# Forty more matmuls on the identity in the first jobs of a fused windowed attention and soft mixture of experts

## The chip, the core and the metric

The kernel runs on one core of one Trainium2 chip. A core has TensorE (PE, matmuls, with its weight loads as PEld), VectorE (DVE), ScalarE (ACT), GpSimd (POOL) and SyncE (SP), which here issues all transfers. Each engine runs its own instructions in order; semaphores order them between engines. Matmuls write to PSUM, from which DVE and ACT copy results to SBUF; GpSimd works on SBUF alone. The metric is device time in microseconds, the median of several executions. The profile is of one execution; its span runs from the first to the last instruction.

## What is computed

Attention with a window of 128 positions and 4 sink positions, then a mixture of experts with soft slots on the attention's result, all in float32:

```python
def _attn_ref(q, k, v, n_sink, window):          # (4, 8, 768, 64) each
    scores = scale * np.matmul(q, k.transpose(0, 1, 3, 2))
    keep = is_sink | in_window
    scores = np.where(keep, scores, -1000000000.0)
    a = np.exp(scores - np.max(scores, axis=-1, keepdims=True))
    a = a / (np.sum(a, axis=-1, keepdims=True) + 1e-09)
    return np.matmul(a, v).astype(np.float32)

def _moe_ref(x, phi, w1, w2):                    # x (3072, 512), w1 (8, 512, 1024), w2 (8, 1024, 512)
    logits = x @ phi                             # 32 slots, 4 per expert
    d = softmax(logits, axis=0)
    slot_input = d.T @ x
    ...
    h = np.maximum(slot_input[e] @ w1[e], 0.0)
    slot_out[e] = h @ w2[e]
    ...
    return (softmax(logits, axis=1) @ slot_out).astype(np.float32)
```

The two softmax calls stand for the lines that are written out in the reference.

## The kernel before

**Tiling.** The attention is cut into 12 jobs: 4 batches by 3 blocks of 256 positions. A job has four score tiles (`softmax`, `tl` 0 to 3: four of the eight heads by one half of the positions in turn). For each job, `prep` transposes the block of k and of q on TensorE and has the halves copied from PSUM to `kt` and `qt` by ACT and DVE; `scores` makes a score tile in an "s" tile of PSUM; `maxima` masks it and takes the negative maxima on DVE; `exps` takes the exponentials on ACT, which gives the "s" tile back; `inverse` (DVE) and a multiplication on GpSimd normalise; `weights_transposed` transposes the weights of two tiles; ACT and DVE copy them to `xw`; `select` cuts the window's triangles out on GpSimd; `sinks_transposed`, `values` and `natural` make the block's output, and `moe.tokens` adds it to the slots' running softmax. In the first job, q and k come in quarters, and `prep` runs in two parts. `sink_values` and `batch_sinks` prepare the sinks' values (one matmul on TensorE, then work on ACT and DVE).

After the last job `moe.finish` closes the slots' softmax, and `tail` runs the experts' two layers on weights that SyncE has loaded into free buffers since the first jobs, and combines them into the output.

**Order.** The steps of `window_path` aren't issued as written. `Plan.add` records each with a key, an engine (or a choice of two), a planned time, what it reads and writes, and the PSUM tiles that it opens and closes. `Plan.order` (a list scheduler) simulates the engines with these planned times and puts each step on its engine's list: at each turn the engine that can start first takes, among the steps that could start nearly then (0.1 on TensorE), the one of the lowest key. `Plan.issue` emits the instructions in that order, and each engine keeps it.

```python
                if e == "P":
                    _, t, i = min((steps[i][0] + self.STAY * (self.modes[i] != mode), t, i)
                                  for t, i in at if t <= t0 + 0.1)
```

A step that opens PSUM tiles starts only when the banks are back. There are four "w" tiles (one bank each; transposes take two at once) and two "s" tiles. A bank comes back `LAT` = 0.25 after the planned end of the step that closes it. A change of TensorE's tile mode costs a planned `SWITCH` = 0.15.

**Fillers.** Three places issue matmuls whose results nobody reads, with counts in `WARM` (line 619). `WARM[0]` = 8 stand at the very start, before any plan (line 1155). `WARM[2]` are for the wait after the last job (lines 959 to 963). `WARM[1]` is what is changed; its steps are made at line 926, before those of the jobs, need nothing, and have key 1000, above every other key of the jobs:

```python
    def busy(e, h, n=P):
        nc.tensor.matmul(h["tile"][:, 0:n], lhsT=c.ident, rhs=c.ident[:, 0:n], start=True, stop=True)


    for _ in range(WARM[1]):
        h = plan.psum()
        add(1000.0, "P", 0.22, lambda e, h=h: busy(e, h), new=h, last=h)
```

So the planner puts one wherever TensorE has no real step within 0.1 and a "w" bank is free, from the plan's start until they are used up. A filler is a 128 by 128 by 128 product in float32: two matmul instructions and two weight loads in the trace.

Of the kernel before, what the change touches and what calls it, by code (L numbers as in the profile page):

```python
# [615 lines left out]


NSLOT = 24
WARM = 8, 10, 64
PT = 3  # L620
CFG = {'prep': [12.61, 9.18],
       'load': [-3.38, -3.85],
# [22 lines left out]
def window_path(ctx, tc, c, moe, q, k, v, phi, w1, w2, out):  # L645
# [279 lines left out]
# [5 lines that stand above are left out]
    for n, (b, j) in enumerate(jobs):  # L930
# [24 lines left out]
        if j == NJ - 1:  # L955
            if b == B - 1:
                moe.finish(plan, [t(x) for x in O["fin"]])

                for _ in range(WARM[2]):
                    h = plan.psum("s")  # L960
# [163 lines left out]
def fused(ctx, tc, q, k, v, n_sink, window, phi, w1, w2, out):  # L1124
# [28 lines left out]
    t = wps.tile([P, 512], F32, name="w")  # L1153
    for _ in range(WARM[0]):
        nc.tensor.matmul(t[:, 0:P], lhsT=c.ident, rhs=c.ident, start=True, stop=True)  # L1155
# [47 lines left out]
```

## Time and profile before

| what | us |
|---|---|
| median of 3 executions | 250.08 (249.75 to 250.85) |
| the profiled execution | 250.21 |
| its span | 248.5 |
| TensorE busy in the span | 216.5 |
| attention's jobs, about | 8 to 190 |
| last matmuls end, about | 239 |

The page gives the busy time of each engine and, in 40 slices of 6.2 us, its busy share in tenths; a row PEclk gives the TensorE clock that was granted, in tenths of the full clock. Most of the instructions carry line 127, which is the helper that keeps the program's order, so groups are told apart by the tiles that they write and read: `s<-wt,qt` are scores, `w<-ident,first` the transposes of k and q, `w<-ident` alone the fillers. Bare `wt` covers several buffers of one pool (`kt`, `xw`, weights and others).

### The profile page before, as it was taken

The page shows a single profiled execution, that of the slowest core. Times are in us where ns is not written, and L with a number is a line of the kernel's source. Part 1 is how long each engine was busy: PE and PEld are TensorE (multiplying, and loading weights), DVE is VectorE, ACT ScalarE, POOL GpSimd, SP SyncE. Part 2 cuts the span into 40 slices and gives each one's busy share as a digit, 9 for nine tenths or more (in the row PEclk, how much of TensorE's full clock was granted, in tenths as well). Part 3 has the DMA queues.
Part 4 walks back from the last instruction along what each step waited for, and adds up shares of the span by engine and source line. Part 5 has one row for each costly group of instructions (what it writes and reads, how often), then busy time and mean ns, then how long its engine had stood idle before and what let it go on. Part 6 is the DMA issues. An engine that isn't in the chain of part 4 may idle for free.

```text
span 248.5 us, 8602 instructions
## 1 busy us (share of the span) xinstructions
PE 216.5 (87%) x3356; PEld 153.7 (62%) x3356; DVE 161.5 (65%) x440; ACT 151.2 (61%) x577; POOL 142.3 (57%) x281
## 2 busy tenths in 40 slices
PE   7865899898999798999979899978999999989830
PEld 7743576675777476676747677656778434746520
DVE  3289569669899947889984888997544512215340
ACT  2167569869788886868897777988645212105230
POOL 2036687977857895976789497669984160000000
PEclk9985799999999999999999999999999999999995
DMA  5497989998799999999989997360159899996996
GB/s 123 107 203 156 173 254 285 282 277 261 224 212 280 280 254 256 266 252 191 277 177 268 282 329 165 68 214 4 44 179 370 307 384 349 348 351 222 340 331 223
DMA packets 102963, 59.44 MB, mean 239 GB/s; under 512 B 76292, under 2 KB 98820, under 8 KB 102916
## 3 DMA queue, kind: packets, MB, share of 16 engines
q1 hardware_dynamic: 102916, 58.83, 85.2%
q8 instruction: 28, 0.46, 0.8%
q14 instruction: 19, 0.16, 0.2%
HBM read 52.53 MB, written 6.29 MB: 237 GB/s over the span
## 4 chain that ended last, share of the span: by engine, by line
PE 52%; DVE 27%; ACT 13%; issue 4%; POOL 0%; ACTq 0%; DVEq 0%; POOLq 0%
PE w L127 34%; PE s L127 16%; DVE wt L127 13%; ACT wt L127 9%; DVE s L127 8%; DVE rs L127 2%; PE w L1155 2%; DVE first L127 1%; ACT wt L580 1%; ACT first L127 1%; DVE call L127 1%; DVE acc L127 1%; DVE sums L127 0%; DVE vsink L127 0%; ACT qt L127 0%
## 5 line engine op out<-in xcount | busy, mean ns | idle before, releaser
L127 ACT ACTIVATE wt<-s,wt 128x132 f32<-128x132 f32 x192 | 68.7, 377 | 10.4 <-DVE wt L127 7.2
L127 POOL TENSOR_TENSOR wt<-wt 128x528 f32<-128x528 f32 x96 | 63.9, 672 | 19.3 <-DVE wt L127 5.9
L127 POOL TENSOR_SCALAR_AFFINE_SELECT wt<-wt 128x512 f32<-128x512 f32 x88 | 54.6, 643 | 15.5 <-DVE sums L127 9.7
L127 PE MATMUL w<-wt 128*64 128x128 f32 (+3 forms) x550 | 50.6, 317 | 1.5 <-DVE wt L565 1.0
L127 PE MATMUL s<-wt,qt 64*64 64x196 f32 (+2 forms) x768 | 43.2, 332 | 9.9 <-ACT wt L127 7.0
L127 PEld LDWEIGHTS w<-wt 128*64 128x64 f32 (+2 forms) x550 | 35.9, 140 | 13.6 <-DVE wt L565 1.5
L127 ACT ACTIVATION_READ_ACCUMULATOR wt<-s,wt 128x1 f32 x192 | 40.6, 211 | 0.0
L127 PEld LDWEIGHTS s<-wt,qt 64*64 64x64 f32 x768 | 27.0, 136 | 20.0 <-ACT wt L127 10.7
L127 DVE TENSOR_REDUCE wt<-s 128x4 f32<-128x528 f32 x48 | 34.0, 707 | 1.7
L127 PE MATMUL w<-ident,wt 64*128 64x64 f32 (+1 forms) x442 | 29.3, 242 | 3.0 <-ACT wt L127 1.1
L127 ACT COPY wt<-w 128x512 f32<-128x512 f32 (+1 forms) x41 | 23.7, 581 | 11.5 <-PE w L127 8.4
L127 PEld LDWEIGHTS w<-ident,wt 64*128 64x128 f32 (+1 forms) x442 | 21.5, 144 | 12.6 <-issue 5.3
L127 DVE COPY wt<-w 128x512 f32<-128x512 f32 (+1 forms) x33 | 22.0, 667 | 10.8 <-PE w L127 10.8
L127 PEld LDWEIGHTS w<-ident,first 64*128 64x128 f32 x576 | 22.2, 143 | 10.8 <-issue 5.0
L127 PE MATMUL w<-ident,first 64*128 64x64 f32 x576 | 27.3, 234 | 1.5 <-ACT first L127 1.5
L127 ACT COPY first<-w 128x512 f32<-128x512 f32 x32 | 18.7, 593 | 15.5 <-PE w L127 15.4
L127 DVE COPY_PREDICATED s<-later,s 128x256 f32<-128x256 uint8 x48 | 20.4, 426 | 4.4 <-PE s L127 3.2
L127 DVE TENSOR_TENSOR wt<-wt 128x4 f32<-128x4 f32 x48 | 13.7, 286 | 10.2 <-ACT wt L127 9.0
L127 ACT ACTIVATE qt<-w 128x512 f32<-128x512 f32 (+1 forms) x25 | 14.4, 580 | 6.8 <-PE w L127 4.8
L127 PE MATMUL s<-wt 128*32 128x256 f32 x256 | 15.4, 381 | 1.0 <-DVE wt L565 1.0
L127 PE MATMUL w<-wt,si 128*32 128x512 f32 x112 | 13.9, 593 | 0.0
L127 POOL COPY wt<-wt 128x512 f32<-128x512 f32 (+2 forms) x13 | 5.7, 457 | 13.5 <-ACT wt L127 10.9
(115 smaller groups left out, 247.4 us busy)
## 6 DMA issues: line engine op xcount, KB each, us to landing
wt<-in_moe_w_dram SPq DMA_DIRECT2D x30, 1024.0 KB, 8.2
wt<-in_v_dram SPq DMA_DIRECT2D x24, 256.0 KB, 5.4
first<-in_q_dram SPq DMA_DIRECT2D x22, 256.0 KB, 5.0
first<-in_k_dram SPq DMA_DIRECT2D x22, 256.0 KB, 4.7
out_dram<-wt SPq DMA_DIRECT2D x4, 1024.0 KB, 7.4
first<-in_moe_w_dram SPq DMA_DIRECT2D x2, 1024.0 KB, 4.9
out_dram<-wt SPq DMA_DIRECT2D x3, 512.0 KB
first<-in_k_dram SPq DMA_DIRECT2D x4, 128.0 KB, 2.3
```

The lines of the kernel that those rows point to most:

```text
L127: return self.tc.keep_in_program_order(f(*args, **kw))
L580: (nc.vector.tensor_copy if n % 2 else nc.scalar.copy)(ob[:, 2 * (n - n0):2 * (n - n0) + 2], yp)
L1155: nc.tensor.matmul(t[:, 0:P], lhsT=c.ident, rhs=c.ident, start=True, stop=True)
```

## The change

One constant: the count of the fillers of the plan goes from 10 to 50. No other step, key or planned time is touched; the order of the other steps comes out of the same planner, run with forty more steps in its list.

```diff
 NSLOT = 24
-WARM = 8, 10, 64
+WARM = 8, 50, 64
 PT = 3
```

## The prediction

> **What bounds the kernel now.** I read the page's head first: busy shares, the granted clock by slices, the chain that ended last.
>
> ```profile
> span 248.5 us, 8602 instructions
> PE 216.5 (87%) x3356; PEld 153.7 (62%) x3356; DVE 161.5 (65%) x440; ACT 151.2 (61%) x577; POOL 142.3 (57%) x281
> ...
> PEclk9985799999999999999999999999999999999995
> ...
> PE 52%; DVE 27%; ACT 13%; issue 4%; POOL 0%; ACTq 0%; DVEq 0%; POOLq 0%
> ```
>
> TensorE is the most used engine, and the chain is on it for half of the span and on DVE for a quarter; no DMA is in it. A slice is 6.2 us, so the digits 8, 5, 7 are a stretch of low clock between about 15 and 30 us, in the first job and the start of the second. The windows view finds its edges and what TensorE did around it (columns: stretch, length, busy time and count of PE, PEld, DVE, ACT, POOL, granted clock, DMA share, GB/s).
>
> ```profile
> 17.30:17.40 0.10, 0.10 (x6) 0.00 (x0) 0.09 (x1) 0.00 (x0) 0.10 (x1) 0.84 1.36 223
> 27.60:27.70 0.10, 0.10 (x6) 0.00 (x0) 0.10 (x1) 0.00 (x0) 0.00 (x0) 0.95 1.02 164
> ...
> 13.96:17.37 3.41, 1.85 (x32) 1.24 (x32) 2.48 (x10) 2.94 (x16) 1.50 (x2) 1.00 1.31 239
> 17.37:20.78 3.41, 2.25 (x31) 1.63 (x28) 3.15 (x13) 1.95 (x10) 1.80 (x5) 0.50 0.99 182
> 20.78:24.20 3.42, 1.71 (x24) 1.44 (x24) 3.35 (x7) 2.56 (x11) 2.45 (x5) 0.50 0.58 132
> 24.20:27.61 3.41, 3.21 (x32) 2.06 (x32) 1.26 (x5) 0.59 (x1) 3.08 (x8) 0.50 1.29 240
> ...
> 164.14:167.56 3.42, 2.30 (x64) 1.66 (x60) 3.35 (x10) 3.19 (x18) 2.70 (x5) 1.00 0.53 149
> ```
>
> The first row is 0.84 on average between 1.0 and 0.5, so the clock halved at 17.37; by the second row it came back at 27.61. In the 3.41 us before the fall TensorE was busy 1.85 us, 54%; it was busy 94% in the 3.41 us before the rise. The last row is the emptiest such stretch that I found with the clock staying up: 67%. So a stretch somewhere between 54% and 67% busy costs the clock, and the fillers act here.
>
> **What the cold stretch costs.** Time at half clock is a loss only where the chain is on TensorE. Two rows split it:
>
> ```profile
> 8.00:24.40 16.40, 10.28 (x151) 7.62 (x151) 12.46 (x37) 9.50 (x41) 6.34 (x12) 0.79 0.74 147
> ...
> 17.37:24.40 7.03, 3.96 (x53) 3.07 (x49) 6.70 (x20) 4.51 (x19) 4.45 (x9) 0.50 0.80 160
> ```
>
> Up to 24.40 DVE is busy 6.70 of 7.03 us. TensorE idles 7.03 - 3.96 = 3.07 us there, cold as it is. A warm TensorE changes nothing as long as DVE's queue is full; DVE is what is late next. From 24.40 it turns round (timeline: start, duration, engine, operation, count, idle time before and its releaser):
>
> ```profile
> 23.67 0.68 DVE L127 COPY wt<-w 128x512 f32<-128x512 f32 x1
> 24.40 3.45 PE L127 MATMUL s<-wt,qt 64*64 64x196 f32 x32 [1.91 <-DVE wt L127]
> 24.43 0.59 ACT L127 COPY wt<-w 128x512 f32<-128x512 f32 x1 [1.01 <-DVE wt L127]
> 25.07 2.26 PEld L127 LDWEIGHTS s<-wt,qt 64*64 64x64 f32 x30 [0.39 <-ACT wt L127]
> 26.71 0.43 DVE L127 COPY_PREDICATED s<-later,s 128x256 f32<-128x256 uint8 x1 [2.08 <-PE s L127]
> 27.17 0.71 DVE L127 TENSOR_REDUCE wt<-s 128x4 f32<-128x528 f32 x1
> 28.00 0.37 ACT L127 ACTIVATE wt<-s,wt 128x132 f32<-128x132 f32 x1 [2.98 <-DVE wt L127]
> 30.05 0.44 PE L127 MATMUL w<-ident,wt 128*128 128x128 f32 x2 [1.05 <-ACT wt L127]
> 30.42 0.89 PE L127 MATMUL s<-wt,qt 64*64 64x196 f32 x16
> ```
>
> These are job 1's first two score tiles, 16 instructions each. They start when DVE has copied half of kt (24.35) and run on when ACT has copied the other (25.02). DVE then waits 2.08 us for the first tile. That wait is cold matmul time, on the path: 26.71 - 25.07 = 1.64 us for the 14 instructions left of tile one. The last row is the same tile warm: 0.89 us for 16, so at most about 0.85 for 14.
>
> **The change, part by part.** WARM[1] goes from 10 to 50: forty more fillers, each two matmul instructions and two weight loads on the identity, no DMA, nothing on another engine. Nobody reads their result. A filler takes one of the four "w" PSUM tiles, and the planner gives it planned TensorE time only where no real step is ready within 0.1.
>
> *Price of one.* Cold and warm, by the fillers that are there:
>
> ```profile
> 1.54 3.78 PE L1155 MATMUL w<-ident 128*128 128x128 f32 x16 [1.54 <-POOL ident masks.py:199]
> 5.12 2.91 PE L127 MATMUL w<-ident 128*128 128x128 f32 x16
> ...
> 8.35 0.52 PEld L127 LDWEIGHTS w<-ident 128*128 128x128 f32 x4
> 8.99 0.45 PEld L127 LDWEIGHTS w<-ident,first 64*128 64x128 f32 x8
> ```
>
> Sixteen instructions, eight fillers, from 1.54 to 5.12: 0.45 us each, cold. Warm: 0.52 / 2 = 0.26.
>
> *How many fit in the first job.* Walking by hand through the scheduler's list (planned 0.22 for a filler, 0.25 more until its bank is back, 0.15 for a change of tile mode) I place 1 before q's first transposes, 3 before the first scores, 7 before the sink values' matmul, 1 between the third and fourth score tile, 7 after q of job 1, 4 before k of job 1, 4 after it: 27. Copies still holding two or three of the banks set these numbers. On the chip the room is 16.40 - 10.28 = 6.1 us of idle, and about 2.0 more when the 3.96 us of cold work run at full clock: 8.1 us, for 27 x 0.26 = 7.0. They fit, closely. The other 13 find no place there and are planned into gaps of later jobs.
>
> *Does the clock stay up?* In 13.96 to 17.37 the seven fillers before the sink values start when that matmul does now and push it to about 14.2, so TensorE is busy until about 14.6, 0.64 us more; with one filler of 0.26 between the score tiles the stretch comes to 1.85 + 0.9 = 2.75 us, 81%, above the 67% that kept the clock. After 17.37 fillers lie in all the large gaps.
>
> *Front.* One filler stands between k's and q's first transposes:
>
> ```profile
> 8.45 0.37 ACT L127 COPY wt<-w 128x256 f32<-128x256 f32 x1 [6.15 <-PE w L127]
> 9.62 0.38 ACT L127 ACTIVATE qt<-w 128x256 f32<-128x256 f32 x1 [0.79 <-PE w L127]
> 10.14 1.56 PE L127 MATMUL s<-wt,qt 64*64 64x68 f32 x32 [0.56 <-ACT qt L127]
> ```
>
> Weight loads end at 8.35 + 0.52 = 8.87 and q starts at 8.99 (ACT's copy gave a bank back at 8.82): 0.12 us of cover for 0.26. So about +0.1 on the scores at 10.14, from which the DVE chain hangs. The three fillers behind it have 0.56 us of idle and the pipeline's drain for 0.78. Bounds: 0 to +0.3; I take **+0.1**. The fillers after that have their gap and do not reach 24.40: k's transposes are needed by DVE only at 23.67.
>
> *Cold scores.* 1.64 less 0.82 to 0.85: **-0.8**. It passes on: DVE spends 27.88 - 26.71 = 1.17 us on a tile, so tile two, warm at about 26.7, is not late; ACT's exponentials at 28.00 wait for DVE, the sink transposes at 30.05 for ACT, then TensorE carries the chain.
>
> *The 13 left over.* Places like these, where the chip idles too:
>
> ```profile
> 41.26:44.68 3.42, 2.39 (x39) 1.51 (x43) 3.29 (x9) 2.90 (x12) 3.19 (x7) 1.00 0.97 241
> 65.16:68.57 3.41, 2.90 (x78) 2.35 (x76) 2.62 (x6) 2.45 (x9) 2.88 (x5) 1.00 0.67 151
> 82.22:85.64 3.42, 2.45 (x50) 1.63 (x46) 3.22 (x12) 3.11 (x14) 2.83 (x5) 1.00 1.00 330
> ```
>
> 1.0, 0.5 and 1.0 us idle, for one or two fillers each. Bounds: 0 if all are covered, 13 x 0.26 = 3.4 if all are on the path. I take two of them: **+0.5**, near the covered end, as the rows show idle time at the planned places. Below nothing isn't excluded either: more fillers shift planned times by tenths, and near ties in the queues of ACT, DVE and GpSimd may be broken otherwise; I give that 1 us either way in the range.
>
> Sum on the profiled execution's 250.21 us (span 248.5 and 1.7 around it): 250.21 + 0.1 - 0.8 + 0.5 = **250.0**, against a median of 250.08.
>
> The Trainium skill, "TensorE: Matmul & The Clock Gate", section "HAM oscillation — how this bites in real kernels", speaks against this: it names idle gaps over about 3.4 us as what drops the clock. Here no gap before the fall is longer than 1.95 us (scores at 15.21, quoted below), so by it idle time isn't the cause and fillers wouldn't save the clock; the trace disagrees as far as a row can, and I follow the trace.
>
> ```profile
> 15.21 0.30 PE L127 MATMUL s<-wt,qt 64*64 64x68 f32 x2 [1.95 <-ACT wt L127]
> ```
>
> **The rivals.**
> 1. *The left-over fillers are on the path* (slower). Place: job 1 and later, where TensorE carries the chain and the chip runs behind the plan (the scores at 30.42 are planned at 27.9), so that a planned gap may be none; price 0.26 each and a bank held. All 13: 250.21 + 0.1 - 0.8 + 3.4 = 252.9; nine of them 251.9. It makes the kernel slower by over 0.5% (above 251.33) from seven on. For it: TensorE's 52% of the chain; against it: the three rows above.
> 2. *The clock falls all the same.* If it falls at 17.37 and rises at 20.78 after a full stretch, the seven fillers after q of job 1 take 3.1 us and push the transposes at 20.69 to about 21.9: +1.2, so 251.2. If it stays low to 27.61, as the skill's rule of gaps would leave it, 15 fillers cost 6.75 us against 3.07 us of idle: 3.7 late, no gain, 250.21 + 0.1 + 3.7 + 0.5 = 254.5. For it: one alignment of stretches is seen. The same page's "Part 1: The HAM clock gate" calls the 3.4 us window free-running, so that other executions would cut it elsewhere; one profile can't show that. Against: with 27 fillers no 3.41 us that I can lay has under 2.4 us busy.
> 3. *More is gained.* All PE work between 17.37 and 27.61 was on the path (7.2 us busy, 3.6 saved): 250.21 + 0.1 - 3.6 + 0.5 = 247.2. For it: the chain does touch transposes there; against: DVE at 6.70 of 7.03.
> 4. *It doesn't do what it says*: gaps closed, clock up, but tile one waits for something else and nothing moves: 250.2 to 250.8.
>
> **How the numbers follow.** Forecast 0.50 (its own range 249.0 to 251.2), rival 1 0.20, rival 2 0.10, rival 3 0.10, rival 4 0.10. A measurement of this kernel tells about 0.5%, 1.25 us, from no change, so faster means under 248.83. Faster: rival 3 and the forecast's lower tail, 0.15. Slower: most of rival 1 and half of rival 2, 0.23. Same: 0.62. Range 248.6 to 252.0: it takes in most of rival 1 and leaves out its worst, the second price of rival 2 and most of rival 3.
>
> **What would show it.** Right: no 5 in the clock's slices after the first job starts; job 1's first pair of score tiles in about 2.4 us rather than 3.45, still starting near 24.5; DVE's wait of 2.08 down to about 1.3; sink transposes near 29.3. The left-over: identity matmuls on "w" after 30 us, with or without an idle gap beside them. Wrong: the clock falls again, the scores of job 1 start over 0.5 us later or earlier than 24.4, or the gain at 30 us differs from that at the end by more than 1 us, which would be the left-over fillers or a changed order.

## The result, and the profile after

The changed kernel takes 275.36 us (median of 4, 274.28 to 276.46), the kernel before 249.92 beside it: a ratio of 1.0986 (95% interval 1.094 to 1.1032), 25 us slower, far outside the predicted range of 248.6 to 252.0. The profiled execution took 276.46 with a span of 274.7. The same rows of the page as were shown of before:

```profile
span 274.7 us, 8716 instructions
PE 234.5 (85%) x3434; PEld 164.4 (60%) x3434; DVE 162.5 (59%) x432; ACT 156.0 (57%) x585; POOL 143.1 (52%) x281
...
PEclk9999999997999999689999995999999999999985
...
PE 64%; ACT 16%; DVE 10%; POOL 3%; issue 3%; POOLq 0%; ACTq 0%
```

The 5 of the first job is gone; the clock stays up through the first job, as forecast, and until about 60 us. New low digits stand in the middle, where before had none, and the chain has moved from DVE to TensorE and ACT. The first job, in the timeline of TensorE of the changed kernel:

```profile
7.68 0.46 PE L127 MATMUL w<-ident,first 64*128 64x64 f32 x8
9.55 1.26 PE L127 MATMUL w<-ident 128*128 128x128 f32 x6
10.74 1.56 PE L127 MATMUL s<-wt,qt 64*64 64x68 f32 x32
23.86 2.03 PE L127 MATMUL w<-ident 128*128 128x128 f32 x14
25.82 1.56 PE L127 MATMUL s<-wt,qt 64*64 64x196 f32 x32
30.12 0.44 PE L127 MATMUL w<-ident,wt 128*128 128x128 f32 x2 [1.59 <-ACT wt L127]
```

The sink transposes start at 30.12, and at 30.05 before. So at 30 us of the program nothing is lost yet, and the 25 us come later. One kind of row marks the pace: `tokens`' logits of jobs 1, 4, 7 and 11 (the last), first of before, then of after (start, duration):

```profile
53.97 1.08 PE L127 MATMUL w<-first,phi 128*32 128x128 f32 x32
96.10 1.08 PE L127 MATMUL w<-first,phi 128*32 128x128 f32 x32
138.25 0.97 PE L127 MATMUL w<-first,phi 128*32 128x128 f32 x28
188.75 0.52 PE L127 MATMUL w<-first,phi 128*32 128x128 f32 x10
```

```profile
57.23 0.97 PE L127 MATMUL w<-first,phi 128*32 128x128 f32 x28
108.09 1.08 PE L127 MATMUL w<-first,phi 128*32 128x128 f32 x32
159.40 0.86 PE L127 MATMUL w<-first,phi 128*32 128x128 f32 x24
214.64 0.62 PE L127 MATMUL w<-first,phi 128*32 128x128 f32 x13
```

Three jobs take 42.1 us before (96.10 - 53.97, 138.25 - 96.10) and 50.9 and 51.3 after, about 9 us more each time, though the timeline of after has one filler in each of these stretches (at 105.47 and 156.78). The last four jobs lose 4.7 more (55.2 against 50.5), and at the last job the loss is 214.64 - 188.75 = 25.9. TensorE's instructions stand in another order from job 1 on.

That order is the planner's. Counting its lists with other values shows a cliff: with 10 to 41 fillers the real steps stand in TensorE's list as before or nearly so, and the planned start of its last real step stays within 189 to 190.4; with 42 it jumps to 208.8, with 50 to 210.3. Of the 50, 40 are planned ahead of 24.1, in the first job, and ten come later. The 42nd is planned in job 0's `tokens`, and this is what it does (planned times, not the chip's):

```
count 41                                  count 42
42.06-42.17 job 0 transpose of lt         42.06-42.17 job 0 transpose of lt
                                          42.66-42.88 filler, holds bank 1 until 43.13
42.95-43.40 job 0 products                43.28-43.73 job 0 products
...                                       ... the same steps, 0.25 later
47.38-47.83 job 2 weights transposed      47.63-48.08 job 2 weights transposed
47.98-50.15 job 1 values, key 29.23       48.23-48.91 job 3 scores, key 1.43
50.30-50.98 job 3 scores, key 1.43        49.06-49.51 job 4 q's transposes
...                                       49.66-51.83 job 1 values, key 29.23
```

With 41, job 3's scores are ready at 47.94. TensorE is free at 47.83 and looks 0.1 ahead, so it misses them by 0.01 and takes the values. With 42, the delay turns GpSimd's list first: at 46.36 the weights that it multiplied there (1.08) aren't ready, and it takes the short copy of job 3's sink keys (0.25) that stood behind them. So the scores are ready at 46.86, and at 48.08 their lower key wins. Then q's transposes of job 4 go ahead of the values, and the lists never come back to the old order.

### The profile page after: what moved, and what is told of

Read it like the earlier page. It is cut to its first block, busy times and chain, and to the rows that moved or that the text cites. A ratio compares the mean times of both kernels' runs of the same rounds, so it can differ in the third digit from the quotient of the medians.

```text
span 274.7 us, 8716 instructions
## 1 busy us (share of the span) xinstructions
PE 234.5 (85%) x3434; PEld 164.4 (60%) x3434; DVE 162.5 (59%) x432; ACT 156.0 (57%) x585; POOL 143.1 (52%) x281
## 4 chain that ended last, share of the span: by engine, by line
PE 64%; ACT 16%; DVE 10%; POOL 3%; issue 3%; POOLq 0%; ACTq 0%
PE w L127 47%; PE s L127 16%; ACT wt L127 10%; DVE wt L127 4%; POOL wt L127 3%; DVE s L127 2%; ACT lt L127 2%; PE w L1155 1%; ACT qt L127 1%; ACT first L127 1%; DVE sums L127 1%; ACT wt L580 1%; DVE rs L127 1%; ACT sums L127 0%; DVE wt L565 0%
## 5 line engine op out<-in xcount | busy, mean ns | idle before, releaser
L127 POOL TENSOR_TENSOR wt<-wt 128x528 f32<-128x528 f32 (+1 forms) x96 | 64.0, 670 | 19.2 <-DVE wt L127 6.8
L127 PE MATMUL w<-wt 128*64 128x128 f32 (+3 forms) x550 | 54.7, 335 | 1.3 <-DVE wt L565 1.0
L127 PEld LDWEIGHTS w<-wt 128*64 128x64 f32 (+2 forms) x550 | 38.5, 150 | 15.0 <-issue 3.4
L127 DVE COPY wt<-w 128x512 f32<-128x512 f32 (+1 forms) x30 | 20.1, 671 | 19.9 <-PE w L127 19.1
L127 PE MATMUL w<-ident,wt 64*128 64x64 f32 (+1 forms) x442 | 27.7, 236 | 3.4 <-ACT wt L127 1.6
L127 ACT COPY wt<-w 128x512 f32<-128x512 f32 (+1 forms) x44 | 25.2, 578 | 8.0 <-PE w L127 6.7
L127 PEld LDWEIGHTS w<-ident,wt 64*128 64x128 f32 (+1 forms) x442 | 20.2, 141 | 11.2 <-issue 5.2
L127 PE MATMUL w<-ident 128*128 128x128 f32 x100 | 17.7, 310 | 0.7 <-DVE wt L127 0.3
L127 DVE TENSOR_TENSOR wt<-wt 128x4 f32<-128x4 f32 x48 | 12.6, 263 | 9.3 <-ACT wt L127 8.2
L127 PEld LDWEIGHTS w<-ident 128*128 128x128 f32 x100 | 14.1, 200 | 3.9 <-DVE first L127 0.9
```

The lines of the kernel that those rows point to most:

```text
L127: return self.tc.keep_in_program_order(f(*args, **kw))
```

## The experiments

Theory "order": the loss is that other order of the real steps, and neither the fillers' work nor their banks on the chip. Rivals: the work of 40 products costs 25 us, or the late fillers alone do.

**One filler more or less.** The line changed is `WARM = 8, 41, 64` and `WARM = 8, 42, 64`.

> Count 41: the fillers that fit in the first job (40) and one more, between q's transposes of job 3 and a score tile of job 2; the order of all other instructions is that of 40, and on TensorE that of the kernel before. Theory 'order' (the loss of 25 us comes from another order of the real steps, which the planner falls into from job 2 on, not from the fillers): 249.5 to 251.0 us, clock never at half after 10 us. Rival 'work' (the 40 added products and the banks that they hold cost 25 us, about 0.6 us each): 31 of 40 are still here, so about 269 us. Rival 'late fillers' (only those behind the first job cost): 1 of 10, 252 us.

> Count 42: one filler more than 41, planned between the transpose and the products of job 0's slot sums, where it delays the products' planned start. From there the planner takes another order. Theory 'order': nearly all of the loss with this one filler, 270 to 276 us. Rival 'work': 0.6 us over the count 41. Rival 'late fillers': 2 of 10, about 255 us.

41 gave 250.93 us, ratio 1.0024 (0.9989 to 1.006); 42 gave 274.86, ratio 1.0959 (1.0873 to 1.1045). One filler costs 24 us, the other 31 added ones nothing that can be told. Rival "work" falls.

**The order without the late fillers, and the late fillers without the order.** The first run plans with 50 and doesn't issue the last ten; the second plans with 40 and issues ten fillers by hand ahead of the same steps.

```diff
             if t > end and self.steps[i][0] >= self.IDLE:
                 continue
+            if self.steps[i][0] == 1000.0 and t > 26.0:
+                continue
```

```diff
+            if i - 40 in self.late and e == "P":
+                for _ in range(self.late[i - 40]):
+                    pool, shape, _ = self.pools["w"]
+                    self.filler({"tile": pool.tile(shape, F32, name="w")})
```

> The order that the planner finds with 50, but its last ten fillers (those planned after 26) are not issued: 40 fillers as with a count of 40. Theory 'order': the loss stays, 272 to 276 us. Rivals 'work' and 'late fillers': it goes with the ten fillers or most of it does, 250 to 255 us.

> The order that the planner finds with 40, with ten fillers put in by hand ahead of the same ten steps that follow them in the changed kernel: the same 50 fillers, the real steps in the old order on TensorE. Theory 'order': 249.5 to 252.5 us (at most 2.6 us for ten fillers of 0.26). Rivals 'work' and 'late fillers': about 275 us.

The order alone: 274.70 us, ratio 1.0975 (1.0879 to 1.1072). All 50 fillers in the old order: 254.60, ratio 1.0163 (1.0072 to 1.0253). So the order carries the loss. The late fillers cost more than expected (252.5 at most): 254.60 - 250.93 = 3.7 us for the nine that the count 41 hasn't, 0.41 each on average, against 0.26 allowed. The work isn't the price: three of them, put in by hand at 57.17, 99.85 and 143.80, wait 1.48 or 1.49 us. A filler reads the identity alone, so it waits for a bank, and the scores behind it wait too.

```profile
99.85 0.49 PE L127 MATMUL w<-ident 128*128 128x128 f32 x2 [1.49 <-DVE wt L127]
```

**No filler at all.** If the order is enough, a change of one planned time that no instruction sees must do the same. In the planner, 0.1 more for job 0's products is past the cliff; here it is TensorE's list that turns, with GpSimd's as before up to there.

```diff
-        plan.add(next(k), "P", 0.45, products, ...
+        plan.add(next(k), "P", 0.55 if n == 0 else 0.45, products, ...
```

> The kernel before (10 fillers, none added); only the planned time of job 0's products goes from 0.45 to 0.55, a number that the planner alone reads. No instruction is added or removed, the order of the real steps changes from job 1 on as with a count of 42. Theory 'order': 270 to 276 us. Rival 'fillers' (their work, their banks on the chip or the clock that they hold up is needed for the loss): 249.5 to 251 us.

273.96 us, ratio 1.0928 (1.0864 to 1.0992), with ten fillers and the same steps as before, of which the planner gives seven more to ACT and seven fewer to DVE. Its page:

```profile
span 272.4 us, 8564 instructions
PE 229.8 (84%) x3358; PEld 159.5 (59%) x3358; DVE 164.8 (60%) x433; ACT 155.8 (57%) x584; POOL 142.6 (52%) x281
...
PEclk9976899986988999689799986988999999999995
```

The clock falls here six times more after the first job. That isn't what makes the loss: the granted clock of the profiled execution is 0.910 here, 0.928 with 42 fillers and 0.954 with the order of 50 without the late ones, and the times are 273.96, 274.86 and 274.70; executions of the kernel before with a granted clock of 0.943 to 0.950 took 251.9 to 253.6. What share of the loss passes through half clock isn't separated: the order of 50 without the late fillers has 14.3 us more idle time of TensorE than count 41 (41.5 and 27.2) and 8.9 us more busy time, some of that at half clock.

**Why the other order is slow.** From job 4 on, q's transposes of a job come after the first score tile of the job before in it; in the old one, after the second, in every third job after the third. The two PSUM tiles of these transposes can only be copied to `qt` when the last scores that read the old `qt` are done. Timeline of before, around one such step (transposes at 81.99 behind a score tile; then ACT's two copies):

```profile
81.16 0.89 PE L127 MATMUL s<-wt,qt 64*64 64x196 f32 x16
81.99 0.71 PE L127 MATMUL w<-ident,first 64*128 64x64 f32 x16
84.48 0.60 ACT L127 ACTIVATE qt<-w 128x512 f32<-128x512 f32 x1 [0.27 <-PE s L127]
87.22 0.90 PE L127 MATMUL s<-wt,qt 64*64 64x196 f32 x16
88.43 0.63 ACT L127 ACTIVATE qt<-w 128x512 f32<-128x512 f32 x1
```

And of after, for the same job:

```profile
84.72 0.89 PE L127 MATMUL s<-wt,qt 64*64 64x196 f32 x16
85.54 0.71 PE L127 MATMUL w<-ident,first 64*128 64x64 f32 x16
90.11 0.60 ACT L127 ACTIVATE qt<-w 128x512 f32<-128x512 f32 x1 [1.01 <-PE s L127]
93.79 0.78 PE L127 MATMUL w<-ident,first 64*128 64x64 f32 x16 [0.71 <-ACT wt L127]
95.81 0.89 PE L127 MATMUL s<-wt,qt 64*64 64x196 f32 x16 [0.98 <-ACT wt L127]
97.20 0.63 ACT L127 ACTIVATE qt<-w 128x512 f32<-128x512 f32 x1
97.89 0.51 PE L127 MATMUL w<-pst,vsink 128*128 128x256 f32 x2 [0.62 <-ACT qt L127]
```

One of the four "w" banks is taken from 81.99 to 89.06, 7.1 us, before; after, from 85.54 to 97.83, 12.3 us. Over jobs 4 to 9 it is 5.0 to 7.1 us before and 12.2 to 13.8 after. The values' first matmul at 97.89 then starts right behind the copy that frees the bank. The view of waits, for TensorE's "w" work (who waited for whom, us, times, longest), before and after:

```profile
PE w L127 <- ACT wt L127: 1.2, 2, 1.1
...
PE w L127 <- ACT qt L127: 0.9, 2, 0.6
```

```profile
PE w L127 <- ACT wt L127: 9.2, 9, 1.6
...
PE w L127 <- ACT qt L127: 4.2, 9, 0.6
```

A wait for a copy can be one for what it writes or for the bank that it frees. It is for the bank alone where the waiting instruction reads nothing that the copy writes: the transposes at 93.79 read `first`, and the copy wrote `wt`; the values at 97.89 read `pst` and `vsink`, and the copy wrote `qt`. From 31 to 190 us the trace of after has 17 such waits, 12.0 us together; that of before has none. So the banks hold up TensorE directly for about half of the loss.

The test: forbid that early step, and nothing else, once with the planned 0.55 and once with the change itself.

```diff
+            held = [("sc", n - 1, 1)] if kind == 1 and n else []
-            hs = transpose(key, src, [("kq", kind, i, y) ...])
+            hs = transpose(key, src, [("kq", kind, i, y) ...] + held)
...
-            w=[sn], new=s, mode=QUARTERS)
+            w=[sn, ("sc", n, tl)], new=s, mode=QUARTERS)
```

> As the run before with 0.55, and the planner may not take q's transposes of a job ahead of the second score tile of the job before it. Theory 'held banks' (the other order is slow because q's transposes run too early and their two PSUM banks stay taken until qt is free for the copy, planned 6.8 against 3.9 on average): the loss goes, 250 to 254 us. Rival 'any other order' (the keys fit one order alone, every other one is slow): 265 us or more, since this order differs from both.

> The changed kernel, 50 fillers, with that same rule for q's transposes. Theory 'held banks': most of the 25 us goes, 253 to 259 us, the rest being the front and late fillers. Rival 'any other order': 270 us or more.

252.56 us, ratio 1.0081 (1.0038 to 1.0123), and 256.29, ratio 1.0233 (1.0172 to 1.0295). The rule takes back 21 of the 23.5 us of the first and 19 of the 25 us of the second, in orders that are neither the old one nor the slow one. The first comes back to the old pattern from job 7 on; the second differs from the old list in half of its places, so "any other order is slow" falls with it. That the bank is the link, and not another effect of the early step, rests on the waits above and on this rule; no run gives the transposes a fifth bank, and what makes the other half of the loss isn't taken apart.

**What the first job gains and loses.** The count 28 keeps all fillers in the first job. Later runs take parts of its added 18 away, in its own plan.

> Count 28: all fillers lie in the first job, 18 more than before; TensorE's order of real steps is that of before. If the clock's fall comes from idle time and costs 0.8 us, as predicted, it stays up and the time is 249.3 to 250.0 us (less about 0.8, plus up to 0.9 at the front, where in the changed kernel the scores came 3.06 us after k's first transposes rather than 2.18). Rival 'worth nothing' (what the clock brings is given back at the front): 250.0 to 250.6. Rival 'the fall has another cause': half clock between about 17 and 28 us again, over 250.6.

> The plan with 28, but the four added fillers ahead of the first scores (one between k's and q's first transposes, three after q's) are not issued; 14 added ones remain. If the front is what eats the clock's gain: the scores start about 2.2 us after k's first transposes instead of 3.06, the clock stays up, and the time is 0.6 to 0.9 us under the count 28, 249.1 to 249.5 us. Rival (the front is covered by something else that comes late, a transfer or DVE's queue): equal to the count 28 within 0.3 us.

> As the run without the front, and only the six fillers ahead of the sink values' matmul (planned 12 to 15) are kept of the added ones. If the stretch just before the fall decides, the clock doesn't fall at 17.4 and this is as good as 14 added fillers, 249.1 to 249.6 us. Rival (the sparse time from 18 to 24 lets it fall in a later stretch of 3.4 us): half clock somewhere in 20 to 28 us, 249.8 us or more.

> Count 28 once more, beside the two before on the same chip: 249.8 to 250.2 us, 0.997 of the kernel before.

> The plan with 28, and none of the 18 added fillers is issued: the instructions of the kernel before, TensorE's order as before, but ACT takes both copies of job 0's first transposed weights and DVE both of job 1's kt, as the planner found with 28. The clock must fall as before. If the 1.2 us by which job 1's scores come nearer to k's first transposes in the two runs without the front (15.26 against 16.44) are this division of copies and not the fillers: 15.3 again, and 248.9 to 249.6 us. If they are the fillers' or the clock's: 16.4 and 250.2 to 250.8 us.

The edit in each is the condition on planned time under which a filler isn't issued:

```diff
+            if self.steps[i][0] == 1000.0 and 8.2 < t < 10.0:                       # no front
+            if self.steps[i][0] == 1000.0 and t > 8.2 and not 12.0 < t < 15.0:      # sinks only
+            if self.steps[i][0] == 1000.0 and t > 8.2:                              # none added
+                continue
```

Runs start k's first transposes at different times, so I measure from there. Rows of the run without the front, then of the run with none added (k's first transposes, first scores, job 1's scores, sink transposes):

```profile
7.14 0.46 PE L127 MATMUL w<-ident,first 64*128 64x64 f32 x8
9.33 1.56 PE L127 MATMUL s<-wt,qt 64*64 64x68 f32 x32 [0.56 <-ACT qt L127]
22.40 0.54 PE L127 MATMUL s<-wt,qt 64*64 64x196 f32 x2 [1.28 <-DVE wt L127]
27.47 0.44 PE L127 MATMUL w<-ident,wt 128*128 128x128 f32 x2 [0.89 <-ACT wt L127]
```

```profile
7.90 0.46 PE L127 MATMUL w<-ident,first 64*128 64x64 f32 x8
10.08 1.56 PE L127 MATMUL s<-wt,qt 64*64 64x68 f32 x32 [0.56 <-ACT qt L127]
23.25 3.68 PE L127 MATMUL s<-wt,qt 64*64 64x196 f32 x32 [0.75 <-DVE wt L127]
29.03 0.44 PE L127 MATMUL w<-ident,wt 128*128 128x128 f32 x2 [0.71 <-ACT wt L127]
```

| run | to first scores | to job 1's scores | to sink transposes | median, us | ratio (interval) |
|---|---|---|---|---|---|
| before (10) | 2.18 | 16.44 | 22.09 | | 1 |
| plan of 28, none added | 2.18 | 15.35 | 21.13 | 249.90 | 0.9966 (0.994 to 0.9993) |
| plan of 28, sinks only | 2.19 | 15.26 | 21.10 | 249.05 | 0.9887 (0.982 to 0.9954) |
| plan of 28, no front | 2.19 | 15.26 | 20.33 | 248.76 | 0.9877 (0.9809 to 0.9944) |
| count 28 | 3.06 | 16.13 | 21.21 | 250.02 | 0.9971 (0.9947 to 0.9996) |
| count 28 again | 3.06 | 16.13 | 21.20 | 250.03 | 0.9947 (0.9901 to 0.9993) |
| changed kernel (50) | 3.06 | 18.14 | 22.44 | 275.36 | 1.0986 (1.094 to 1.1032) |

The steps from 22.09 to 22.44, each the difference of two rows of the table, are these. With the plan of 28 and no added filler, the sink transposes come 0.96 us nearer: the planner lets ACT make both copies of job 0's first transposed weights, so that DVE gets to `kt` sooner; its step on `vsink` also takes 0.66 us there and 1.26 before, for a reason that stays open. Rows of the count 28 (before, DVE copied one of those and one half of `kt`, and was on `kt` from 23.67):

```profile
22.06 1.07 ACT L127 COPY wt<-w 128x512 f32<-128x512 f32 x2
22.63 0.66 DVE L127 TENSOR_TENSOR vsink<-wt,bm 128x512 fp32r<-128x512 f32 x1
23.21 1.48 DVE L127 COPY wt<-w 128x512 f32<-128x512 f32 x2
```

The fourteen fillers that keep the clock up bring 0.80 more (21.13 - 20.33). The four fillers at the front cost 0.88 (21.21 - 20.33). The twelve that 40 has over 28 cost 1.23 (22.44 - 21.21). With the six before the sink values alone, the clock falls one stretch later and nothing of the 0.80 is left:

```profile
17.37:20.78 3.41, 1.49 (x31) 1.06 (x28) 3.15 (x13) 2.20 (x10) 1.80 (x5) 1.00 1.18 218
20.70:20.80 0.10, 0.10 (x2) 0.10 (x4) 0.10 (x1) 0.10 (x1) 0.10 (x1) 0.93 1.29 238
```

The medians follow this more loosely than the rows. The run with sinks only should lie near the one with none added by its rows, and its interval takes in 0.994; but it was faster than its rival allowed (249.05, not 249.8 or more) though the clock fell. The run without the front was a little faster than forecast and the one with none added a little slower, each by 0.3 us. The run without the front is the fastest here, 1.2% under before.

## Why the prediction was wrong

- **What bounds the kernel, and the clock.** Right. Filled idle time keeps the clock up, the same plan without the fillers loses it (none added: digits 9, 9, 8, 5, 7), and the price that was put on it, 0.8, was measured as 0.80 from rows, in the plan of 28. In the changed kernel none of it was left: the sink transposes came 0.35 us later from k's first transposes (22.44 against 22.09).
- **How many fit.** 27 were placed by hand in the first job, with 13 left over; there are 30 and 10. Close in number, but four counted after k of job 1 are seven, 23.86 to 25.82, and they run into job 1's scores: at 25.82 instead of 24.40. "The fillers after that have their gap and do not reach 24.40" was wrong. So was its ground, that DVE needs k's transposes only at 23.67: in the changed kernel DVE waited 0.89 us for them, to 24.04.

```profile
24.04 1.49 DVE L127 COPY wt<-w 128x512 f32<-128x512 f32 x2 [0.89 <-PE w L127]
```

- **Front.** Mis-sized: +0.88 for the +0.1 taken and the +0.3 that was its upper bound. Three fillers behind q's transposes take 1.19 us (9.55 to 10.74), not 0.78; 0.26 for one filler, from weight loads alone, was too low there (seven in a row take 1.96 us, 0.28 each).
- **The leftover fillers.** In the old order 3.7 us for nine: the term of +0.5 was mis-sized, and its upper bound of 3.4 for thirteen too, because both counted a filler's work and not its wait for a bank. Rival 1 named this mechanism, but it isn't the loss of the changed kernel.
- **The step that failed** is one sentence: "near ties in the queues of ACT, DVE and GpSimd may be broken otherwise; I give that 1 us either way". The mechanism is named there, but it was worth 24 us, not 1, and the list on which the loss is made, TensorE's own, is missing. With 42 a near tie on GpSimd's list does turn first; what costs is the choice that follows on TensorE's, between a score tile of key 1.43 and values of key 29.23, and with the planned 0.55 it turns without GpSimd's. The list was treated as an order that fillers are put into; it is made anew with them. A filler is skipped over by key when something real is ready, but holds a bank for 0.47 planned us and so moves what comes ready next.
- **Rivals.** None had the planner's order as its mechanism; only the last sign of being wrong mentions "a changed order". Rivals 2 (the clock falls all the same) and 3 (more is gained on TensorE) fall with the rows of the first job. Rival 4's outcome, nothing gained, is what count 41 shows (250.93), but by another way: the gain is spent at the front and ahead of job 1's scores.

## What to carry to other kernels

When an order comes from a greedy list scheduler, an added step that does nothing is a change of every later decision. Bound it by the spread of planned ends for neighbouring counts and planned times, not by the step's own duration, or put fillers in after the order is fixed. The plan knew it here: its last real step on TensorE starts at 189.1 before, at 191.0 and 194.4 in the two runs with the rule, and at 207.8 to 210.3 in the slow ones, and the medians follow it (250, 252.56, 256.29, 274 to 275.4). A filler put in after the ordering still needs a bank that is free on the chip, as the three that waited 1.5 us show. Where a step is taken early only because its inputs are there, look at what it holds until its output can be drained: here a PSUM bank for 12.3 us rather than 7.1.

## What the runs showed of the hardware

- In each trace the clock's falls and rises lie whole multiples of 3.41 us apart, and what TensorE did in such a stretch goes far to tell what comes at its end. While the attention ran, the clock fell behind stretches with 38% to 58% busy and stayed up behind all with 59% or more; between 53% and 57%, four stayed up, so the share alone doesn't decide there. At half clock, stretches with up to 84% left it low, and 93% or more brought it back. The rows: 58%, fell, and 53%, stayed (changed kernel); 64%, stayed (count 28); 84%, stayed low, and 93%, rose (count 42).

```profile
160.14:163.55 3.41, 1.98 (x48) 1.39 (x37) 2.24 (x7) 1.80 (x7) 1.03 (x2) 1.00 0.00 0
27.02:30.43 3.41, 1.82 (x46) 1.29 (x35) 2.88 (x7) 2.36 (x12) 1.65 (x5) 1.00 1.01 223
...
20.50:23.91 3.41, 2.18 (x39) 1.90 (x38) 3.24 (x10) 3.27 (x14) 2.38 (x4) 1.00 0.71 153
...
111.28:114.69 3.41, 2.87 (x33) 2.09 (x33) 0.95 (x5) 3.36 (x20) 2.91 (x5) 0.50 0.89 270
80.56:83.97 3.41, 3.19 (x20) 1.71 (x21) 3.22 (x7) 1.91 (x7) 3.18 (x7) 0.50 0.99 293
```

- The longest gap doesn't tell it. In before no gap ahead of the fall was over 1.95 us, and ahead of no fall in any trace, while the attention ran, was one over 2.17. The Trainium skill, "TensorE: Matmul & The Clock Gate", section "HAM oscillation — how this bites in real kernels", names idle gaps over about 3.4 us as what drops the clock; these runs don't bear that condition out.
- The same sixteen fillers at the start let k's first transposes begin at 6.76 us in one run (order of 50 without the late fillers) and at 8.03 in another (count 28 again). At first their instructions start 0.21 us apart, later 0.11, and the change comes at 4.6 us in the one and at 7.3 in the other, each on the grid of 3.41 us of that run's later falls. So an execution's grid alone moves the start of the work by over a microsecond, as much as most terms of the prediction. The last eight of the sixteen, in the one and in the other:

```profile
4.88 1.95 PE L127 MATMUL w<-ident 128*128 128x128 f32 x16
```

```profile
5.11 2.99 PE L127 MATMUL w<-ident 128*128 128x128 f32 x16
```

- In the slow order three profiled executions with a granted clock of 0.910, 0.928 and 0.954 took 274.17, 275.22 and 273.99 us: there more time at half clock cost nothing that can be told. In the order of before it did: 251.9 to 253.6 us at 0.943 to 0.950, and 249.6 to 251.5 at 0.956 to 0.975.
